# A fused recurrence and highway layer on one core: PSUM banks of the last unit, output products split in two, and a new hand-written order

## The chip, the cores and the metric

The kernel runs on one core of one Trainium2 chip. The metric is the device time of one execution in microseconds. The core has five engines that matter here: TensorE (PE; its weight loads are listed apart as PEld), VectorE (DVE), ScalarE (ACT), GpSimd (POOL) and SyncE (SP), which here only issues DMA transfers. Each engine takes its instructions strictly in the order in which they are written and waits on semaphores for what it needs.

## What is computed

The reference, cut to what matters, has two stages. The first is a gated recurrence along the sequence, for 4 sequences of 6336 steps and 256 channels:

```python
sig = 1 / (1 + exp(-f_logit))
f = lower_bound + (1 - lower_bound) * sig
h = f[:, t] * h + (1 - f[:, t]) * x[:, t]      # for each t; y[:, t] = h
```

The second is a highway layer on the 25344 x 256 result y:

```python
H = maximum(y @ w_h, 0)
T = sigmoid(y @ w_t + b_t)
out = T * H + (1 - T) * y
```

Inputs and outputs are float32. The kernel computes out as y + T * (max(y, y @ w_h ...) - y) in a rearranged form with scaled weights, in 16-bit types on the engines.

## The kernel before

The 25344 tokens are cut into 28 units: units 0 and 1 have 2 blocks of 128 tokens, unit 2 has 4, units 3 to 25 have 8, unit 26 has 4 and unit 27 has 2. The 256 channels are two halves of 128.

Nothing in the code loops over units. A long string, `order` (L48), lists tokens such as `s3.1:0`; the loop at the end (L385 to L394) takes them one by one and calls `do_` plus the letter. In `s3.1:0`, s is the step, 3 the unit, 1 the half or part, and 0 the buffer slot; `a0` and `a1` name one-bank PSUM slots, a bare 0, 1 or 2 for a product names a slot of two PSUM banks; a trailing `v` puts the step on VectorE; `*3` puts three idle matmuls ahead. All is pinned to this order on each engine, so the string fixes the order of each engine's queue and of SP's transfers. The steps of a unit are:

- l, x (L247 to L251): load logits and x, issued by SP. wt, wh: load weights. w (L380): store, issued by SP.
- u (L253, ACT): u = sigmoid(-logit) over the whole unit.
- b (L259): the product u * x in two parts; POOL, or DVE with `v`.
- i (L268, PE): transpose u to PSUM; f (L274): f = 1 - c * u from there; ACT, or DVE with `v`.
- p (L285, PE): transpose the products b to PSUM. Its one instruction set covers both parts of b.
- s (L304, DVE): the scan, y = f * y + b, each half continuing the half of the unit ahead.
- g and z (`ffn`, L312, PE): the two matmuls of the layer for one half m of the output channels; t (L331, ACT): sigmoid of z; d (L335, DVE): the maximum of g and scaled y, written as d.
- e (L340): d = d * t; POOL, or DVE with `v`. In units 7 to 21 it is one instruction, else two or three parts.
- o (L355, PE): the output product, which turns tokens back into rows: for each block and half a matmul of y with a diagonal matrix (L365) and one of d with the identity (L366), summed in PSUM. c (L369): copy to SBUF; ACT, or DVE with `v`.
- k (L224, PE): idle matmuls on zeros. cc, dg, WT, WH, cb (DVE): preparation of constants and weights. pc, pb (PE): their transposes.

The helper `shared` (L178) keeps the last product b or e (or weight preparation) of VectorE in mind, and makes the next b or e of GpSimd in the list wait for it; it makes VectorE wait for nothing.

Output products of units 24 to 26 are cut into parts of two blocks and those of unit 27 into parts of one block (`part`, L351); others have four blocks.

Of the kernel before, what the change touches and what calls it, by code (L numbers as in the profile page):

```python
# [48 lines left out]
l1:0 l0:1 x0:0 x1:1 k*3:a0 l2:2 wt wh x2:2 l3:3 x3:3 l4:4 pc:0 x4:4 u0:0 l27:1 l5:5 b0.0v:0 x27:0 x5:5 u1:1 cc l6:0
k*3:1 i0.1:0 f0.1:0 dg i1.0:1 b1.0v:1 f1.0:1 k*3:1 k*3:a0 p0.1:1 s0.1:0 i0.0:0 u2:0 f0.0v:0 p0.0:1 s0.0 x6:1 l7:2  # L50
k*3:a0 WT pb:0 k*3:a1 i2.0:0 p1.0:1 f2.0:0 WH k*3:1 s1.0:1 i2.1:0 b2.1v:0 g0.0:1 b2.0 i1.1:1 z0.1:2 f2.1:1 cb f1.1v:2
z0.0:0 g0.1:a0 p1.1:1 t0.0:0 d0.0:0 k*3:1 d0.1 p2.0:0 s1.1 k*3:0 e0.0v z1.1:1 p2.1:1 t0.1 u3:0 l8:3 g1.1:0 x7:2 s2.0:2
e0.1 d1.1:1 b3.0:0 z1.0:2 t1.0:0 i3.1:0 f3.1:0 o0.0:0 g1.0:2 c0.0:0 s2.1 d1.0 b3.1v g2.1:2 i3.0:0 d2.1:0 p3.1*3:1 t1.1
e1.1 e1.0 k*2:0 w0.0 u4:1 z2.0:1 f3.0:1 z2.1:0 b4.0:1 s3.1:0 p3.0:0 o1.0:2 t2.1:0 u27:0 b4.1 c1.0:1 s3.0 w1.0 x8:3
i4.0:1 g2.0:0 f4.0:0 d2.0 i4.1:1 p4.0:0 l9:1 x9:4 l11:4 t2.0 u5:2 e2.1v e2.0v z3.0:0 g3.1:1 b27.0:0 z3.1:2 s4.0:1
p4.1:0 f4.1:1 i5.0:1 t3.0:0 t3.1 d3.1:1 b5.0:2 g3.0:0 f5.0:0 s4.1 o2.0:1 u6:1 b5.1 c2.0:2 d3.0 w2.0 i5.1:1 x11:0 e3.2
g4.1:2 p5.0:0 d4.1:0 b6.0:1 f5.1:1 s5.0:2 z4.1:0 t4.1:1 p5.1:1 b6.1 u7:2 e3.1 s5.1 l10:0 z4.0:1 t4.0 g4.0:0 i6.0:0
e3.0v p6.0:1 d4.0 o3.0:1 e4.2 b7.0:2 f6.0:0 s6.0:3 e4.0v i6.1:0 b7.1 u8:3 f6.1:1 o3.1:0 c3.0:0 c3.1:1 w3.1 w3.0 g5.0:2
p6.1:0 i8.1:1 z5.0:1 f8.1:0 x10:1 e4.1 t5.0:0 g5.1:0 i7.1:1 b8.0:1 s6.1 i7.0:0 d5.0:1 z5.1:1 l12:2 f7.1:1 p7.1:1 d5.1
f7.0:2 t5.1 b8.1 g6.0:2 p7.0:0 e5.1 k*3:0 o4.1:1 s7.1:0 z6.0:0 d6.0:2 s7.0 u9:1 b9.0:2 g6.1:2 c4.1:3 d6.1 i9.0:1  # L60
t6.0:1 b9.1 o4.0:1 u11:2 i9.1:0 f9.0v:1 c4.0:2 w4.0 e6.0v f9.1:2 g7.1:0 z6.1:2 k*3:1 e5.2v i8.0:1 z7.0:1 e5.0v t6.1
w4.1 f8.0:3 p8.1:0 d7.1:0 t7.0:0 g7.0:2 e6.1 p8.0:1 b11.0:3 o5.0:0 u10:1 c5.0:0 w5.0 x12:2 o5.1:1 c5.1:1 w5.1 s8.1:1
i11.1:0 z7.1:0 f11.1:0 s8.0 b11.1 l13:0 d7.0 p9.0:1 i10.1:0 z8.0:1 e6.2 b10.1:1 g8.1:2 t7.1 f10.1:3 p9.1:0 s9.0:2
o6.1:0 x13:0 i10.0:1 d8.1:1 s9.1 g8.0:2 t8.0:1 u12:3 o6.0:1 f10.0:1 c6.1:0 c6.0:2 b10.0 e7.0 i11.0:1 w6.0 p10.0:0 w6.1
f11.0:2 z8.1:0 t8.1 z9.0:1 t9.0:0 d8.0 g9.0:2 s10.0:3 i12.0:1 p10.1:0 l14:1 f12.0:1 d9.0:2 o7.0:0 g9.1:1 c7.0:1 x14:1
w7.0 s10.1 u13:1 o7.1:2 c7.1:3 w7.1 b12.0:2 l17:0 p11.0:1 d9.1 s11.0:0 z9.1:0 t9.1 i12.1:0 b12.1 l15:2 z10.1:1 g10.1:2
e8.0 t10.1:2 e9.0v b13.0:1 z10.0:0 f12.1:2 p11.1:1 b13.1 t10.0 o8.1:1 d10.1:0 p12.1:0 c8.1:0 o8.0:2 s11.1 u14:2
g10.0:0 d10.0 c8.0:2 b14.1:3 i13.1:1 e10.0 f13.1:0 g11.1:1 b14.0 z11.1:0 s12.1:1 d11.1:1 w8.0 t11.1:0 x15:0 w8.1
z11.0:2 i13.0:1 p12.0:0 s12.0 o9.0:0 t11.0 f13.0:2 g11.0:1 d11.0 o9.1:2 e11.0 p13.0:1 c9.0:1 u17:1 i14.0:0 f14.0v:1
c9.1:3 g12.0:0 u15:3 d12.0:2 b15.1:2 w9.0 z12.1:1 i17.0:0 f17.0:3 t12.1:1 o10.0:2 s13.0:2 o10.1:0 p13.1:0 c10.0:0  # L70
s13.1 b15.0 c10.1:1 i14.1:1 g12.1:1 z12.0:2 g13.0:0 i15.0:0 l16:1 f14.1:2 d12.1 p14.0:1 x16:2 d13.0:0 t12.0 o11.0:1
w9.1 g13.1:2 s14.0:3 f15.0:0 p14.1:0 o11.1:0 e12.0 w10.0 w10.1 i15.1:1 c11.0:2 u16:2 x17:1 b16.1:1 b16.0 z13.0:1 d13.1
f15.1:1 c11.1:0 z13.1:2 s14.1 t13.1:0 l18:0 t13.0 w11.0 p15.0:1 o12.1:0 i16.0:0 g14.1:2 s15.0:0 d14.1:1 e13.0 o12.0:1
p15.1:1 s15.1 c12.1:1 b17.1:2 f16.0:2 z14.1:0 z14.0:2 p16.0:0 s16.0:1 c12.0:3 t14.1:1 t14.0 g14.0:1 d14.0 i16.1:1
w11.1 l19:1 u18:3 x18:0 b17.0 e14.0 g15.1:0 d15.1:2 z15.0:2 i17.1:0 x19:3 f16.1:0 b18.0:3 p16.1:1 f17.1:1 b18.1 l20:2
s16.1 o13.1:1 t15.0:0 p17.0:0 g15.0:0 w12.1 d15.0 c13.1:0 u19:1 b19.1:1 o13.0:2 p17.1:1 z15.1:1 c13.0:2 z16.0:0
s17.1:2 t15.1 t16.0:1 z16.1:2 s17.0 g16.0:1 w13.1 t16.1 i18.0:1 d16.0:0 g16.1:0 o14.0:2 i18.1:0 f18.0:0 d16.1 e15.0v
o14.1:1 p18.0:1 s18.0:3 u20:2 w12.0 z17.0:0 c14.0:0 c14.1:1 f18.1:1 g17.0:2 d17.0:1 z17.1:1 b19.0 t17.0:0 i19.1:0
f19.1:0 p18.1:1 o15.1:0 w13.0 s18.1 t17.1 x20:1 i19.0:0 l21:0 g17.1:2 e16.0 d17.1 o15.0:1 f19.0:2 b20.0:2 b20.1
p19.1:0 x21:2 w14.0 i20.1:1 c15.1:2 g18.1:0 w14.1 s19.1:0 c15.0:3 z18.0:1 f20.1:1 l22:1 o16.0:2 d18.1:2 w15.1 u21:1  # L80
t18.0:1 p19.0:0 c16.0:0 i20.0:1 g18.0:0 s19.0 f20.0:0 o16.1:1 c16.1:1 z18.1:2 i21.1:0 b21.1:1 p20.0:1 t18.1 e17.0v
d18.0 o17.0:1 w15.0 z19.1:0 b21.0 f21.1:2 g19.0:2 s20.0:1 x22:0 d19.0:0 p20.1:0 s20.1 c17.0:2 t19.1:0 o17.1:1 u22:2
e18.0 z19.0:0 g19.1:2 b22.1:2 c17.1:3 t19.0 i21.0:1 d19.1 e19.0 i22.0:0 b22.0 f21.0:0 g20.1:1 z20.1:0 l23:2 w16.0
f22.0v:1 d20.1:1 w16.1 w17.0 x23:1 p21.1:1 w17.1 l24:0 u23:1 b23.0:3 t20.1:1 o18.0:2 o18.1:1 c18.0:0 s21.1:2 c18.1:1
p21.0:0 z20.0:0 b23.1 g20.0:2 i22.1:1 x24:2 t20.0 s21.0 f22.1:2 o19.1:1 p22.1:0 d20.0 c19.1:2 e20.0 i23.1:1 z21.0:0
g21.1:1 f23.1:0 t21.0:0 u24:2 p22.0:1 g21.0:2 b24.0:1 s22.1:3 i23.0:0 d21.1:2 f23.0:2 o19.0:0 z21.1:1 b24.1 s22.0
p23.1:0 d21.0 c19.0:3 t21.1 i24.0:1 w18.1 z22.0:0 z22.1:2 g22.1:1 s23.1:0 e21.0 w18.0 f24.0:1 w19.1 d22.1:0 l25:1
i24.1:1 x25:0 t22.0:1 t22.1 f24.1:0 e22.1 p23.0:0 o20.0:0 c20.0:0 w19.0 g22.0:1 p24.1:1 o20.1:2 u25:1 b25.0:2 s23.0
b25.1 p24.0:0 c20.1:1 d22.0 z23.0:0 s24.0:1 g23.0:1 t23.0:2 e22.0 l26:0 o21.0:2 c21.0:2 o21.1:0 s24.1 i25.1:0 g23.1:2
c21.1:3 x26:1 e22.2 g24.1:0 d23.0:1 f25.1:1 u26:2 b26.0:1 i27.1:1 i25.0:0 f27.1:0 d23.1 w20.0 z23.1:1 p25.0:1 f25.0:2  # L90
d24.1:2 s25.0:2 z24.0:2 p25.1:0 b26.1 t23.1 o22.0:0 e23.1 o22.1:1 t24.0:0 e23.2 z24.1:2 c22.0:0 s25.1 w20.1 g24.0:0
d24.0 e23.0v w21.0 c22.1:1 t24.1 w21.1 e24.0 w22.0 i26.0:1 e24.1 z25.0:1 i27.0:0 f26.0:2 g25.0:2 e24.2 i26.1:1 d25.0:0
f27.0:1 t25.0:1 p26.0:0 f26.1:3 o23.0:0 g25.1:1 z25.1:2 p26.1:1 s26.0:3 d25.1 c23.0:0 s26.1 w22.1 o23.1:0 p27.0:0
t25.1 w23.0 c23.1:1 o24.0:1 e25.0v o24.3:2 s27.0:0 g26.0:a1 o24.2:0 c24.0:2 o24.1:1 d26.0:1 c24.3:0 c24.2 c24.1
p27.1:0 e25.1 e25.2v z26.0:2 o25.0:0 o25.1:1 z26.1:a1 s27.1 g26.1:a0 t26.0:0 z27.0:2 c25.0:3 t26.1 c25.1v o25.2:0
t27.0:1 o25.3:1 d26.1 g27.0:a0 w23.1 z27.1:a1 w24.1 w24.0 e26.0 c25.2:0 e26.1v o26.0:2 o26.1:0 d27.0:0 g27.1:a0 d27.1
w25.0 c25.3 t27.1 e27.0 e27.1v o27.0:1 c27.0v:1 c26.0:2 o27.1:a0 c26.1 w25.1 w26.0 w27.0 c27.1:3 w27.1
"""

    NU = len(units)  # L100
# [210 lines left out]

    def ffn(n, m, name, k, slot):  # L312
        N = tokens(n)
        p = two_banks(slot, name)
        for ki in range(NH):
            w = w_sb[:, k, ki, m * P:(m + 1) * P]
            for a in range(0, N, 512):
                e = min(a + 512, N)
                if a == 0:
                    pin(nc.tensor.matmul(p[:, a:e], w, half(n, "y", ki)[:, a:e], start=ki == 0, stop=ki == NH - 1))  # L320
# [31 lines left out]
        w = min(2 if n in (24, 25, 26,) else 4, store(n))  # L352
        return k * w, min(k * w + w, units[n][0])

    def do_o(n, k, eng, slot):  # L355
# [4 lines left out]
        for j in range(a, c):  # L360
            lo = j0 * P + j - j0
            cols = slice(lo, lo + g * (P - 1) + 1, g)
            for h in range(NH):
# [2 lines left out]
                pin(nc.tensor.matmul(o, half(n, "d", h)[:, cols], ident_b, start=False, stop=True))  # L366
# [56 lines left out]
```

## Time and profile before

| | |
|---|---|
| three runs | 207.75, 207.75 and 211.6 us, median 207.75 |
| profiled execution | 207.88 us |
| its span | 206.1 us |
| granted TensorE clock | 0.995 |

The page of a profile gives the busy time of each engine with its share of the span; a busy time is the time in which at least one instruction of the engine was running. A timeline row gives the start in us, the length in us, engine, line, operation, output and inputs with their shapes, the number of instructions merged into the row, and in brackets the idle time ahead of it with the instruction that ended it. A row of the chain that ended last starts with the start and the length. SPq is the issuing queue of SP; a row of issues gives the count, the KB of each, and the median us from issue to landing.

### The profile page before, as it was taken

How to read it: one execution, taken by the hardware profiler on the slowest of the kernel's cores; microseconds unless marked ns; L12 is line 12 of the kernel's file. 1: busy time of each engine (PE TensorE's matmuls, PEld its weight loads, DVE VectorE, ACT ScalarE, POOL GpSimd, SP SyncE). 2: the span in 40 equal slices, each digit the busy share in tenths (PEclk: the TensorE clock that was granted, in tenths of full speed). 3: DMA queues.
4: the chain of work that ended last, by engine and by line, in shares of the span. 5: the costliest groups of instructions: out<-in, count | busy, mean ns of one | idle time of the engine just before them, and what ended most of it. 6: DMA issues, size and time to landing. Idle time of an engine off the chain costs nothing.

```text
span 206.1 us, 4635 instructions
## 1 busy us (share of the span) xinstructions
PE 192.6 (93%) x1837; PEld 133.8 (65%) x1837; DVE 194.5 (94%) x159; ACT 191.9 (93%) x192; POOL 173.8 (84%) x93
## 2 busy tenths in 40 slices
...
GB/s 196 370 424 422 411 418 423 409 423 417 414 423 408 429 417 426 423 420 413 425 424 416 433 411 417 429 415 418 407 422 422 414 392 378 286 104 204 138 382 248
DMA packets 16125, 78.68 MB, mean 382 GB/s; under 512 B 1764, under 2 KB 2536, under 8 KB 10216
## 3 DMA queue, kind: packets, MB, share of 16 engines
...
q8 instruction: 14, 0.23, 0.4%
...
HBM read 52.43 MB, written 25.95 MB: 380 GB/s over the span
## 4 chain that ended last, share of the span: by engine, by line
PE 53%; ACT 14%; DMA 13%; DVE 10%; issue 6%; POOL 2%; SPq 1%; ACTq 0%; DVEq 0%; POOLq 0%
DMA x<-in_x_dram 9%; DVE y L308 8%; PE op L366 7%; PE bT L291 7%; PE op L365 7%; PE g L320 7%; PE z L320 6%; PE uT L271 6%; PE g L114 6%; PE z L114 6%; ACT o L378 4%; ACT f L282 4%; DMA out_dram<-o 4%; ACT t L333 3%; POOL bv L264 2%
## 5 line engine op out<-in xcount | busy, mean ns | idle before, releaser
L264 POOL TENSOR_TENSOR bv<-u,x 128x1024 bf16<-128x1024 f16 (+1 forms) x49 | 100.9, 2085 | 16.9 <-DVE bt L207 10.7
L308 DVE TENSOR_TENSOR_SCAN y<-f,y,bT 128x1024 bf16<-128x1024 f16 (+5 forms) x54 | 106.8, 1989 | 0.2 <-PE bT L291 0.2
L343 POOL TENSOR_TENSOR d<-d,t 128x512 bf16<-128x512 bf16 (+3 forms) x33 | 73.3, 2234 | 9.6 <-DVE d L343 4.2
L337 DVE SCALAR_TENSOR_TENSOR d<-y,ncc,g 128x1024 bf16<-128x1024 bf16 (+2 forms) x56 | 63.1, 1137 | 1.5 <-PE g L320 1.0
L333 ACT ACTIVATE t<-z,bt 128x1024 bf16<-128x1024 f32 (+2 forms) x56 | 58.9, 1088 | 1.3 <-PE z L114 0.7
L282 ACT ACTIVATE f<-uT,ncc 128x1024 f16<-128x1024 f16 (+2 forms) x51 | 55.4, 1098 | 3.4 <-PE uT L271 2.2
L378 ACT COPY o<-op 128x1024 f32<-128x1024 f32 (+2 forms) x55 | 52.1, 984 | 2.4 <-PE op L366 1.6
L256 ACT ACTIVATE u<-l 128x2048 f16<-128x2048 f32 (+2 forms) x28 | 49.8, 1781 | 2.8 <-DMA l<-in_f_logit_dram 2.7
L366 PE MATMUL op<-ident_b,d 128*128 128x128 bf16 x396 | 49.5, 219 | 0.6 <-DVE d L343 0.6
L365 PE MATMUL op<-diag,y 128*128 128x128 f16 x396 | 49.7, 219 | 0.1
L366 PEld LDWEIGHTS <-d 128*128 128x128 bf16 x396 | 44.0, 113 | 3.2 <-DVE d L343 0.7
L365 PEld LDWEIGHTS <-y 128*128 128x128 bf16 x396 | 44.2, 113 | 1.7
L320 PE MATMUL g<-y,w_sb 128*128 128x512 bf16 (+1 forms) x112 | 39.5, 367 | 0.9 <-DVE d L337 0.7
L320 PE MATMUL z<-y,w_sb 128*128 128x512 bf16 (+1 forms) x112 | 39.3, 367 | 0.4 <-ACT o L378 0.4
L291 PE MATMUL bT<-ident_f,bv 128*128 128x128 f32 x198 | 31.8, 277 | 4.3 <-DVE y L308 2.6
L114 PE MATMUL z<-y,w_sb 128*128 128x512 bf16 x92 | 34.9, 379 | 0.0
L114 PE MATMUL g<-y,w_sb 128*128 128x512 bf16 x92 | 34.9, 379 | 0.0
L320 PEld LDWEIGHTS <-w_sb 128*128 128x128 f16 x224 | 21.6, 98 | 17.5 <-issue 0.9
L271 PEld LDWEIGHTS <-u 128*128 128x128 f16 x396 | 26.3, 98 | 10.2 <-issue 2.6
L271 PE MATMUL uT<-ident_h,u 128*128 128x128 f16 x396 | 31.2, 220 | 1.6 <-DVE y L308 0.8
L291 PEld LDWEIGHTS bT<-ident_f,bv 128*128 128x128 f32 x198 | 22.4, 141 | 12.3 <-ACT f L282 3.0
L114 PEld LDWEIGHTS <-w_sb 128*128 128x128 f16 x184 | 18.0, 98 | 16.7 <-issue 1.8
...
## 6 DMA issues: line engine op xcount, KB each, us to landing
...
l<-in_f_logit_dram SPq DMA_DIRECT2D x23, 1024.0 KB, 12.0
x<-in_x_dram SPq DMA_DIRECT2D x23, 1024.0 KB, 13.4
...
```

Source lines behind the costliest of these rows:

```text
L114: return pe.add_instruction(mybir.InstMatmult(name=nc.get_next_instruction_name(), start_tensor_calc=start, stop_tensor_calc=stop, tile_si ...
L264: shared(pin(e.tensor_mul(st[n]["bv"][:, a:c].rearrange("p k d j -> p k j d"), st[n]["u"][:, 2 * a:2 * c].rearrange("p (k j) d -> p k j d" ...
L271: pin(nc.tensor.transpose(uT[:, j * P:(j + 1) * P], st[n]["u"][:, j, h * P:(h + 1) * P], ident_h))
L282: pin(nc.scalar.activation(to, of, AF.Identity, scale=ncc[:, h:h + 1], bias=1.0))
L291: pin(nc.tensor.transpose(words[:, k:k + g * (P - 1) + 1:g], pair, ident_f))
L308: pin(nc.vector.tensor_tensor_scan(y[:, c:e], st[n]["f", h][:, c:e], st[n]["bT", h][:, c:e], 0.0 if fresh else carry[h], op0=ALU.mult, op1 ...
L320: pin(nc.tensor.matmul(p[:, a:e], w, half(n, "y", ki)[:, a:e], start=ki == 0, stop=ki == NH - 1))
L333: pin(nc.scalar.activation(half(n, "t", m), st[n]["z", m][:, :tokens(n)], AF.Sigmoid, bias=bt[:, m:m + 1]))
L337: pin(nc.vector.scalar_tensor_tensor(half(n, "d", m), half(n, "y", m), ncc[:, m:m + 1], st[n]["g", m][:, :tokens(n)], op0=ALU.mult, op1=AL ...
L343: shared(pin(e.tensor_mul(st[n]["d"][:, a:c], st[n]["d"][:, a:c], st[n]["t"][:, a:c])), not eng)
L365: pin(nc.tensor.matmul(o, half(n, "y", h)[:, cols], diag[:, h], start=True, stop=False))
L366: pin(nc.tensor.matmul(o, half(n, "d", h)[:, cols], ident_b, start=False, stop=True))
```

## The change

Three things in the code:

- `ffn`: in unit 27 both halves m of a gate product (g or z) share one PSUM tile; half m takes its columns m * 256 to m * 256 + 256, so both lie in one bank. Before, each half had a tile of its own.
- A new step q holds the y matmuls of an output product in units 25, 26 and 27, and o then holds only the d matmuls; in the other units o holds both as before. The first matmul into a bank alone has the start flag in q. The loop over halves is now outside the loop over blocks, in all units.
- The string `order` is replaced by a new one. It has 829 tokens where the old has 821; the eight more are the q tokens. Engines change for some tokens: b1.0 and b2.1 go from VectorE to GpSimd, b3.0 and b4.1 from GpSimd to VectorE; e0.0, e2.0, e2.1, e4.0, e25.2 and e27.1 from VectorE to GpSimd, e1.1, e3.1, e4.1, e4.2 and e27.0 from GpSimd to VectorE; f0.1, c25.0, c25.3, c26.0 and c27.1 from ScalarE to VectorE, c25.1 from VectorE to ScalarE. All other tokens keep their engine.

The diff, with the middle of the new string left out:

```diff
+l0:0 x0:0 l1:1 x1:1 k*3:a0 wh pc:0 pb:1 l2:2 u0:0 x2:2 b0.0v:0 wt cc k*3:2 l3:3 dg x3:3 l4:0 i0.1:0 x4:0 l5:4 i0.0:1
+f0.0v:0 k*3:0 p0.0:1 u1:1 x5:4 l27:1 f0.1v:1 b1.0:1 cb k*3:a0 p0.1:0 s0.0:0 k*3:0 s0.1 i1.1:1 f1.1v:0 p1.1:0 u2:0 WH
+b2.0:0 b2.1 k*2:0 l6:5 i1.0:1 k*3:1 f1.0:1 g0.1:0 g0.0:1 p1.0:1 s1.1:1 d0.1:0 i2.0:0 s1.0 d0.0 WT f2.0:0 g1.1*2:0
+i2.1:1 d1.1:1 f2.1:1 g1.0:1 p2.0:0 z0.1:2 p2.1:1 t0.1:0 u3:0 s2.0:2 z1.0:0 z1.1:2 e0.1 d1.0 s2.1 z0.0:1 k*3:a0 i3.1:0
+b3.1v:0 b3.0v t1.0:1 i3.0:1 t1.1 e1.1v g2.1:0 t0.0 f3.1:0 p3.1*1:0 f3.0:1 d2.1:2 s3.1:3 e0.0 z2.0:1 u4:0 o0.0:0 t2.0:0
+e1.0 c0.0:0 w0.0 z2.1:2 i4.0*1:1 x6:1 p3.0:0 g2.0:0 f4.0:2 l7:0 o1.0:1 t2.1 i4.1:1 k*3:2 c1.0:1 b4.1v:1 b4.0 s3.0 x7:2
+f4.1:0 u5:1 w1.0 l8:2 k*3:1 d2.0 p4.0:1 e2.1 z3.1:1 t3.1:1 g3.1:0 s4.0:0 z3.0:2 d3.1:0 e2.0 p4.1:0 i5.0:1 s4.1 u27:0
+b5.1:0 g3.0:1 x8:3 l9:3 d3.0 o2.0:0 b5.0 e3.2 e3.1v t3.0 e3.0v f5.0:1 u6:2 i5.1:1 p5.0:0 g4.1:2 c2.0:0 w2.0 f5.1:0
+x9:0 b6.0:1 s5.0:1 z4.1:1 t4.1:0 d4.1:1 o3.0:0 c3.0:2 u7:1 i6.0:1 g4.0:1 f6.0:1 p5.1:0 w3.0 o3.1:0 z4.0:2 s5.1 b6.1
+i6.1:1 c3.1:1 d4.0 w3.1 p6.0:0 f6.1:0 g5.0:0 t4.0 l11:0 p6.1:1 s6.0:2 k*3:1 s6.1 b7.1:0 z5.0:2 u8:2 b7.0 x11:1 i7.0:0
+t5.0:1 z5.1:1 e4.0 g5.1:2 d5.0:0 l10:1 b8.1:1 t5.1 b8.0 d5.1 g6.0:1 d6.0:2 e5.2v e4.1v e5.0v x27:4 p7.0:1 e4.2v f7.0:0
+u9:3 s7.0:3 i8.1:0 z6.1:0 g6.1:2 f8.1:1 x10:5 i7.1:0 z6.0:1 t6.1:2 f7.1:2 o4.1:0 l12:4 t6.0 i8.0:0 d6.1 c4.1:0 b9.1:2
+f8.0:0 p7.1:1 s7.1 o5.1:1 o4.0:0 c5.1:1 i9.0:0 f9.0v:2 c4.0:2 b9.0 w4.0 e6.1 w4.1 e6.2 e6.0v e5.1 k*3:2 z7.1:1 p8.0:1
+w5.1 s8.0:0 u11:1 i9.1:0 g7.1:0 d7.1:1 z7.0:2 b11.0:0 b11.1 f9.1:3 b27.0:3 p8.1:0 t7.1:0 t7.0 s8.1 x12:0 g7.0:1 d7.0
+u10:2 o5.0:2 i11.1:1 o6.1:0 p9.0:0 f11.1:0 s9.0:1 c5.0:3 i10.1:1 f10.1:1 z8.0:1 g8.1:2 w5.0 t8.0:1 l13:0 i10.0:1
...
+c22.1:1 b26.1 t24.1 z25.0:1 e23.1 p26.0:0 g25.0:2 e23.2 f27.0:0 i26.0:1 z25.1:0 e23.0v d25.0:0 t25.0:1 g25.1:1 f26.0:1
+s26.0:2 i26.1:1 o23.0:2 w21.0 e24.0 w21.1 p26.1:0 t25.1 o23.1:0 d25.1 f26.1:3 p27.0:1 e24.1 w22.0 c23.0:0 s26.1
+o24.0:1 e24.2 c23.1:2 s27.0:3 o24.1:2 w22.1 g26.0:a0 c24.0:1 e25.0v o24.2:0 p27.1:1 o24.3:1 c24.1 c24.2:3 g26.1:2
+d26.0:1 z26.0:a0 s27.1 d26.1 c24.3 q25.1:0 w23.0 t26.0:0 q25.0:a1 e25.1 o25.1 o25.0 e25.2 q25.3:1 z26.1:a0 w23.1
+c25.0v:0 o25.3 c25.1 w24.0 q25.2:0 e26.0 c25.3v:2 t26.1 g27.1:2 o25.2 w24.1 z27.1:a1 c25.2 e26.1v z27.0 d27.1:0
+q26.0:a0 w25.0 q26.1:1 t27.1:0 o26.0 w25.1 t27.0 c26.0v:1 o26.1 g27.0 e27.1 d27.0 q27.1:0 e27.0v c26.1 q27.0:a1 o27.1
+c27.1v:0 w26.0 o27.0 w27.1 c27.0v:3 w27.0
...
     def ffn(n, m, name, k, slot):
         N = tokens(n)
-        p = two_banks(slot, name)
+        if n in (27,):
+            if name not in st[n]:
+                st[n][name] = two_banks(slot, name)
+            p = st[n][name][:, m * N:(m + 1) * N]
+        else:
+            p = two_banks(slot, name)
...
-    def do_o(n, k, eng, slot):
-        op = two_banks(slot, "op").rearrange("p (j d) -> p j d", d=D)
+    def outputs(n, k, op):
         a, c = part(n, k)
         j0, j1 = blocks(n, a // store(n))
         g = j1 - j0
-        for j in range(a, c):
-            lo = j0 * P + j - j0
-            cols = slice(lo, lo + g * (P - 1) + 1, g)
-            for h in range(NH):
-                o = op[:, j - a, h * P:(h + 1) * P]
-                pin(nc.tensor.matmul(o, half(n, "y", h)[:, cols], diag[:, h], start=True, stop=False))
-                pin(nc.tensor.matmul(o, half(n, "d", h)[:, cols], ident_b, start=False, stop=True))
+        for h in range(NH):
+            for j in range(a, c):
+                lo = j0 * P + j - j0
+                yield (h, j) == (0, a), (h, j) == (NH - 1, c - 1), op[:, j - a, h * P:(h + 1) * P], h, slice(lo, lo + g * (P - 1) + 1, g)
+
+    def do_q(n, k, eng, slot):
+        op = two_banks(slot, "op").rearrange("p (j d) -> p j d", d=D)
+        for first, _, o, h, cols in outputs(n, k, op):
+            pin(nc.tensor.matmul(o, half(n, "y", h)[:, cols], diag[:, h], start=first, stop=False))
+        st[n]["op", k] = op
+
+    def do_o(n, k, eng, slot):
+        if n in (25, 26, 27,):
+            for _, last, o, h, cols in outputs(n, k, st[n]["op", k]):
+                pin(nc.tensor.matmul(o, half(n, "d", h)[:, cols], ident_b, start=False, stop=last))
+            return
+        op = two_banks(slot, "op").rearrange("p (j d) -> p j d", d=D)
+        for _, _, o, h, cols in outputs(n, k, op):
+            pin(nc.tensor.matmul(o, half(n, "y", h)[:, cols], diag[:, h], start=True, stop=False))
+            pin(nc.tensor.matmul(o, half(n, "d", h)[:, cols], ident_b, start=False, stop=True))
         st[n]["op", k] = op
```

77 lines of the change are left out of this document (28 added, 49 removed).

## The prediction

> **What bounds the kernel now.** I read the page first (engine totals), then busy time by stage, then VectorE's timeline, because the totals point at it, and last the issues and the queue of SP. Columns of the stage row: PE, PEld, DVE, ACT, POOL busy, granted clock, DMA share, GB/s.
>
> ```profile
> PE 192.6 (93%) x1837; PEld 133.8 (65%) x1837; DVE 194.5 (94%) x159; ACT 191.9 (93%) x192; POOL 173.8 (84%) x93
> 30.00:170.00 140.00, 135.19 (x1324) 95.58 (x1323) 139.43 (x92) 139.58 (x128) 132.87 (x57) 1.00 1.02 418
> ```
>
> The second line is the argument: from 30 to 170 us DVE stands still for only 140.00 - 139.43 = 0.57 us and ACT for 0.42 us, while DMA is full too. DVE's queue never runs dry, so what is added to DVE before the tail is added to the end, and what is taken from it is taken from the end, unless a gap appears or closes. ACT loses work by the change, so I sum on DVE: time to its first work, its instructions, its waits, and what follows the last. The profiled execution took 207.88 us for a span of 206.1, so 1.8 us lie around the span; the median of the runs shown is 207.75, 0.13 less. The matmul count and the warming matmuls of the k tokens (35 in each list) stay, apart from one more on another token, so PE's total stays.
>
> Here are the rows of DVE from which prices come. A step is the start of the next row less the start of this one, since neighbours overlap by some 0.1 us.
>
> ```profile
> 5.52 0.73 DVE L264 TENSOR_TENSOR bv<-u,x 128x512 bf16<-128x512 f16 x1 [4.39 <-DMA x<-in_x_dram]
> ...
> 12.06 0.71 DVE L264 TENSOR_TENSOR bv<-u,x 128x512 bf16<-128x512 f16 x1
> 12.67 0.14 DVE L207 COPY bt<-tbT 128x2 f32<-128x2 f32 x1
> 12.73 0.47 DVE L280 TENSOR_SCALAR f<-uT,ncc 128x256 f16<-128x256 f16 x1
> 13.12 0.89 DVE L337 SCALAR_TENSOR_TENSOR d<-y,ncc,g 128x256 bf16<-128x256 bf16 x2
> ...
> 14.59 0.27 DVE L343 TENSOR_TENSOR d<-d,t 128x256 bf16<-128x256 bf16 x1
> 14.78 1.27 DVE L308 TENSOR_TENSOR_SCAN y<-f,y,bT 128x512 bf16<-128x512 f16 x1
> ...
> 17.96 1.75 DVE L264 TENSOR_TENSOR bv<-u,x 128x1024 bf16<-128x1024 f16 x1
> 19.61 0.73 DVE L337 SCALAR_TENSOR_TENSOR d<-y,ncc,g 128x512 bf16<-128x512 bf16 x1
> 20.33 4.58 DVE L308 TENSOR_TENSOR_SCAN y<-f,y,bT 128x1024 bf16<-128x1024 f16 x2
> 24.83 0.72 DVE L337 SCALAR_TENSOR_TENSOR d<-y,ncc,g 128x512 bf16<-128x512 bf16 x1
> 25.47 0.78 DVE L343 TENSOR_TENSOR d<-d,t 128x512 bf16<-128x512 bf16 x2
> 26.17 2.34 DVE L308 TENSOR_TENSOR_SCAN y<-f,y,bT 128x1024 bf16<-128x1024 f16 x1
> ...
> 42.76 0.67 DVE L343 TENSOR_TENSOR d<-d,t 128x1024 bf16<-128x1024 bf16 x1
> 43.34 2.34 DVE L308 TENSOR_TENSOR_SCAN y<-f,y,bT 128x1024 bf16<-128x1024 f16 x1
> ```
>
> Steps: b of 512 elements 0.61; f of 256 0.39; e of 256 0.19, of 512 0.35 (0.70 for two), of 1024 0.58; d of 512 0.72 and 0.64; two scans 4.50, so 2.25 each; b of 1024 1.65. That last price is doubtful, as two more products of this form come to DVE:
>
> ```profile
> 12.91 1.17 POOL L264 TENSOR_TENSOR bv<-u,x 128x512 bf16<-128x512 f16 x1 [10.67 <-DVE bt L207]
> 15.00 0.68 POOL L343 TENSOR_TENSOR d<-d,t 128x256 bf16<-128x256 bf16 x1 [0.92 <-DVE d L343]
> 16.40 2.14 POOL L264 TENSOR_TENSOR bv<-u,x 128x1024 bf16<-128x1024 f16 x1 [0.72 <-DMA x<-in_x_dram]
> ...
> 21.39 4.25 POOL L264 TENSOR_TENSOR bv<-u,x 128x1024 bf16<-128x1024 f16 x2 [0.23 <-DMA x<-in_x_dram]
> ```
>
> POOL's own product of the same unit ran until 16.40 + 2.14 = 18.54, across the first 0.58 us of DVE's 1.75. Twice the 512 step is 1.22; 1.22 + 0.58 would be 1.80, near the 1.75. So I price a 1024 product at 1.2 where POOL is quiet, with 1.65 as its other end.
>
> The Trainium skill, "SBUF — State Buffer", section "Who interferes with whom", says that a VectorE instruction with two SBUF inputs and a GpSimd instruction that reads SBUF exclude each other for the whole instruction. By that rule DVE begins at 18.54 and the sum takes 1.2, which the 0.58 us above agrees with; if the rule did not act here the sum would take 1.65.
>
> **Start, up to the scans of unit 3.** The new list issues l0, x0 ahead of l1, x1. So x0 is SP's second issue and not its third:
>
> ```profile
> 1.16 0.42 SPq L244
> ...
> 1.63 3.79 DMA x<-in_x_dram
> ```
>
> Issued at 1.16 with the same 3.79 us, x0 lands at 4.95, and DVE begins 0.5 us earlier than 5.52. From its start to b3.1v DVE spent 17.96 - 5.52 = 12.44. On this stretch the new list takes b1.0, b2.1 and e0.0 off DVE (0.61 + 0.61 + 0.19 = 1.41) and puts f0.1 on it (0.39): 11.42, so b3.1v would come at 16.4 (4.95 + 11.42). The other end: the first f and p steps pass PE behind more k groups, and the loads land as before; 0.6 us more gives 17.0. Earlier than 16.40 is excluded: x3, still the tenth load, is what POOL's row at 16.40 waited for. I take 16.4. b1.0, b2.0 and b2.1 now run on POOL, which stood idle until 12.91; b1.0 waits there for the dg instructions and b2.0 for those of WH, since the new list puts those just ahead, and p2.0 follows. That is the work most likely to add the 0.6.
>
> Then b3.1v and b3.0v, both on DVE. POOL is quiet: the next product there, e0.0, stands behind e1.1v, for which the helper makes it wait. 16.4 + 1.2 + 1.2 + 0.19 (e1.1v) + 0.72 (d2.1) = 19.7 for s3.1, against 20.33 before: -0.6. With 1.65 twice it is 20.6, +0.3.
>
> **Units 3 to 6.** DVE gains b4.1v (1.2) and e3.1v, e4.1v, e4.2v (3 x 0.35 = 1.05), and loses e2.1, e2.0 (0.70) and e4.0 (0.58): +0.97, or +1.42 at the dear price. What is queued behind b4.1v: x4 landed by 21.39, b4.1v comes at 19.7 + 2.25 = 21.95, so no load holds it. b4.0 on POOL now waits for b4.1v: 21.95 + 1.2 = 23.15, plus half of POOL's 4.25 for two, gives 25.3, and p4.0 follows. DVE covers this with s3.0 (2.25) and d2.0 (0.64), until 26.04; 0.7 us of cover for the transposes, half of it needed. If u4 is late, each us of it goes through to s4.0. Sum to unit 7: -0.6 + 0.97 = +0.35 (ends +0.3 and +2.3: 17.0 for 16.4, 1.65 three times).
>
> **Middle.** Units 7 to 24 have the same DVE instructions in another order. The gaps can shrink by 0.57 at most. To the other side the nearest rows are DVE's waits in the tail below, of which the longest is 0.78; two such are 1.6. I take 0, since every token here keeps its engine. The order of output products is now half by half in all units; the same matmuls in another order, and each is covered by the DVE row beside it; without cover it would show as one such wait.
>
> **Tail.** Rows of DVE from s26.1, and the last copy on ACT:
>
> ```profile
> 192.98 1.27 DVE L308 TENSOR_TENSOR_SCAN y<-f,y,bT 128x512 bf16<-128x512 f16 x1
> 194.17 0.66 DVE L343 TENSOR_TENSOR d<-d,t 128x1024 bf16<-128x1024 bf16 x1
> 194.75 0.73 DVE L308 TENSOR_TENSOR_SCAN y<-f,y,bT 128x256 bf16<-128x256 f16 x1
> 195.41 0.72 DVE L337 SCALAR_TENSOR_TENSOR d<-y,ncc,g 128x512 bf16<-128x512 bf16 x1
> ...
> 197.35 0.69 DVE L376 COPY o<-op 128x512 f32<-128x512 f32 x1 [0.23 <-PE op L366]
> ...
> 199.06 0.42 DVE L343 TENSOR_TENSOR d<-d,t 128x512 bf16<-128x512 bf16 x1
> 199.61 0.48 DVE L337 SCALAR_TENSOR_TENSOR d<-y,ncc,g 128x256 bf16<-128x256 bf16 x1
> 200.87 0.48 DVE L337 SCALAR_TENSOR_TENSOR d<-y,ncc,g 128x256 bf16<-128x256 bf16 x1 [0.78 <-PE g L320]
> 201.46 0.29 DVE L343 TENSOR_TENSOR d<-d,t 128x256 bf16<-128x256 bf16 x1
> 202.07 0.43 DVE L376 COPY o<-op 128x256 f32<-128x256 f32 x1 [0.32 <-PE op L366]
> ```
>
> ```profile
> 202.63 0.37 ACT L378 COPY o<-op 128x256 f32<-128x256 f32 x1 [1.30 <-PE op L366]
> ```
>
> From s26.1 to the end of the last copy: 203.00 - 192.98 = 10.02. Removed: the 0.78, in which g27.1 waited for the bank that d27.0 was reading (both had slot a0). In the new list both gate products share slot 2, and g27.0 stands behind o26.1. Added to DVE: three copies net (c25.0, c25.3, c26.0 and c27.1 for c25.1); e25.2 leaves for POOL. New DVE sequence: s26.1 1.19, e25.0 0.58, s27.0 0.66, s27.1 0.66, d26.0 and d26.1 0.67 each, c25.0, c25.3 and c26.0 0.69 each, e26.1 0.42, d27.1 and d27.0 0.48 each, e27.0 0.29, c27.1 and c27.0 0.43 each: 9.03. Waits that stay: 0.32 for the last output product and one like the 0.23 where c25.3 follows e25.2 on POOL. Sum 9.6: -0.4. The y products issued ahead leave only the d products after the last e; but that 0.32 is mostly the first product's way, so I cut nothing for them. Ends: -0.9 with no waits (9.03), and +0.4 if the 0.78 comes back elsewhere.
>
> The Trainium skill, "PSUM — Partial Sum Buffer", section "PSUM bank collisions raise a hardware error", has accesses of two engines kept apart by bank, not by address. That speaks against one bank for both halves: g27.0 must then follow d27.1's read, and t27.1 must follow z27.0. No row here shows a bank shared in this way.
>
> By rows: d27.1 follows e26.1 on DVE and takes 0.48, about as long as o26.0 and o26.1 need on PE after the same e26.1, so g27.0 loses at most some tenths; the +0.4 end holds it.
>
> **Sum.** 207.88 + 0.35 + 0 - 0.4 = 207.83, taken as 207.8, which is 0.05 above the median of the runs.
>
> **The rivals.** (1) Slower, by the price of DVE's products and by the start: a 1024 product costs 1.65 whether or not POOL reads, and PE's early groups cost 0.6. For it: 1.65 is the only measured step. Against it: the 512 steps. 207.88 + 2.3 - 0.4 = 209.8; it decides against the forecast from a product of some 1.5 us on. (2) Slower by more: SP, in order, now has store w0.0 ahead of load x6, where ten further loads stood ahead of it.
>
> ```profile
> 13.82 0.33 SPq L244 DMA_DIRECT2D l<-in_f_logit_dram  x1
> ...
> l<-in_f_logit_dram SPq DMA_DIRECT2D x23, 1024.0 KB, 12.0
> x<-in_x_dram SPq DMA_DIRECT2D x23, 1024.0 KB, 13.4
> ```
>
> The issue at 13.82 is l6; what is in flight then lands 12.0 to 13.4 us later, at about 26. SP stands until c0.0 on ACT is done, which needs e0.0 on POOL (after e1.1v, so 19.0 + 0.68) and stands behind u4 and t2.0.
>
> ```profile
> 18.77 1.91 ACT L256 ACTIVATE u<-l 128x2048 f16<-128x2048 f32 x1
> 20.59 1.10 ACT L282 ACTIVATE f<-uT,ncc 128x1024 f16<-128x1024 f16 x1
> ```
>
> u4 was at 18.77; the new list puts f3.0 (1.10) ahead of it, so it ends near 21.7 (18.77 + 1.10 + a step of 1.82), and t2.0 and c0.0, each half as wide as that f, bring c0.0 to 23 or 24. Below 26 the queue keeps DMA full; beyond it each us is a us without loads, felt by DVE once b6 is late. The same pattern returns with w3.1 and w5.0 ahead of loads. With c0.0 at 31, or two holes of half that, 207.8 + 5 = 212.8. (3) Faster: the new order closes the 0.57 and the tail's waits: 207.88 + 0.3 - 0.57 - 0.9 = 206.7. (4) The shared bank and the early y products do nothing, as the last e still ends the chain: tail 0, 208.2.
>
> **How the numbers follow.** Forecast 0.45 (own range 207.2 to 208.6, holding rival 4 too, 0.08), rival 1 0.18, rival 2 0.13, rival 3 0.16. The range 206.4 to 210.8 takes in all but rival 2 and the tips of 1 and 3. Two per cent, about what a measurement of this kernel can tell from no change, is 4.2 us: 203.6 and 211.9. Faster than 203.6 would need more than all the gaps here: 0.03. Slower than 211.9 is rival 2 and a part of rival 1: 0.14. Within: 0.83.
>
> **What would show it.** In the new profile: DVE's first product near 5.0; b3.1v at 16.4 to 17.0, the two products there at 1.25 us each and s3.1 near 19.7; DVE idle from 30 to 170 us below 1.2; SP's issue of x6 before 26 and DMA share 1.0 to 170; some 9.6 us from s26.1 to the last copy, with no wait of 0.78 before a d of 256. Wrong if DVE shows a gap in the middle, above all one ended by a load or by POOL's b; then the queue's order decided and not DVE's sum.

## The result, and the profile after

The changed kernel takes 210.25 us (median of 4 runs, 209.97 to 210.44) against 207.99 for the kernel before, taken beside it: ratio 1.0108, 95% interval 1.0093 to 1.0123. It is slower by 1.1%: inside the range and inside two per cent, but 2.45 us above the 207.8 forecast. With an interval 0.3% wide, far less than the two per cent that the prediction allowed can be told from no change here. The profiled execution took 209.97 us with a span of 208.0, 1.9 more than the 206.1 of before.

The engine totals and the stage from 30 to 170 us, columns as before:

```profile
PE 192.8 (93%) x1811; PEld 134.0 (64%) x1838; DVE 197.1 (95%) x162; ACT 191.0 (92%) x188; POOL 173.9 (84%) x94
```
```profile
30.00:170.00 140.00, 134.28 (x1298) 95.19 (x1317) 139.89 (x94) 139.81 (x128) 132.20 (x55) 1.00 1.02 418
```

DVE's gaps in the middle shrank from 0.57 to 0.11 us, and nothing new opened there. A gap doesn't show a row that has grown, so the place of the loss is read from the starts of rows. DVE's start:

```profile
4.16 0.73 DVE L265 TENSOR_TENSOR bv<-u,x 128x512 bf16<-128x512 f16 x1 [3.03 <-DMA x<-in_x_dram]
...
16.40 2.47 DVE L265 TENSOR_TENSOR bv<-u,x 128x1024 bf16<-128x1024 f16 x2
18.75 0.29 DVE L349 TENSOR_TENSOR d<-d,t 128x256 bf16<-128x256 bf16 x1
...
19.68 2.35 DVE L309 TENSOR_TENSOR_SCAN y<-f,y,bT 128x1024 bf16<-128x1024 f16 x1
21.95 1.30 DVE L265 TENSOR_TENSOR bv<-u,x 128x1024 bf16<-128x1024 f16 x1
23.16 2.32 DVE L309 TENSOR_TENSOR_SCAN y<-f,y,bT 128x1024 bf16<-128x1024 f16 x1
25.41 0.71 DVE L343 SCALAR_TENSOR_TENSOR d<-y,ncc,g 128x512 bf16<-128x512 bf16 x1
26.44 2.35 DVE L309 TENSOR_TENSOR_SCAN y<-f,y,bT 128x1024 bf16<-128x1024 f16 x1 [0.32 <-PE bT L292]
```

b3.1v at 16.40, the two products in 2.35 (1.18 each), s3.1 at 19.68 and b4.1v at 21.95 are where the forecast had them. The miss begins in the last row, at s4.0, which waits for p4.0. The tail:

```profile
193.68 1.91 DVE L309 TENSOR_TENSOR_SCAN y<-f,y,bT 128x512 bf16<-128x512 f16 x2
...
199.21 0.69 DVE L394 COPY o<-op 128x512 f32<-128x512 f32 x1 [1.09 <-DMA out_dram<-o]
200.54 0.69 DVE L394 COPY o<-op 128x512 f32<-128x512 f32 x1 [0.63 <-ACT t L339]
...
204.09 0.76 DVE L394 COPY o<-op 128x256 f32<-128x256 f32 x2 [0.66 <-DMA out_dram<-o]
```
```profile
199.19 0.59 ACT L396 COPY o<-op 128x512 f32<-128x512 f32 x1 [0.92 <-DMA out_dram<-o]
```
```profile
198.86 0.39 PE L379 MATMUL op<-ident_b,d 128*128 128x128 bf16 x4
```

Three copies, c25.0v, c25.1 on ACT and c27.1v, wait by these rows for a store, not for a product. The 0.63 ahead of c25.3v is probably a fourth wait of this kind, though its row names a sigmoid: its product o25.3 (the PE row) was done at 199.25, and its buffer, slot 2, waits for the store w23.1, issued at 195.1. s26.1 starts 0.70 us later than before (193.68 against 192.98); from there to the last copy it takes 204.85 - 193.68 = 11.17 us against 10.02 (+1.15); from the last copy to the end of the span 3.15 against 3.1. That is the whole 1.9. The chain of work that ended last runs through two of these waits, both for one buffer:

```profile
192.97 1.03 ACT o L396
...
194.02 5.08 DMA out_dram<-o
...
199.21 0.70 DVE o L394
...
199.97 4.03 DMA out_dram<-o
...
204.09 0.09 DVE o L394
```

The third part of a token c is the slot of the output buffer in SBUF, 0 to 3. c23.0 fills slot 0 and its store w23.0 takes 5.08 us; c25.0v has slot 0 too; its store w25.0 takes 4.03; c27.1v has slot 0 again. In the old list the buffers went round in another order (c24.3 had slot 0, c25.0 slot 3, c27.0 slot 1).

My theory after this: (a) the tail is late by these buffers, (b) the start by the 0.39 us at s4.0 and the products added to DVE, which nothing behind it gives back. Rivals: the waits for stores stand only ahead of other waits; the store w0.0 ahead of x6 starves the loads; ACT or the loads, as full as DVE, set the pace.

### The profile page after: what moved, and what is told of

Same layout as the page of the kernel before. It is cut to its first block, busy times and chain, and to the rows that moved or that the text cites. A ratio compares the mean times of both kernels' runs of the same rounds, so it can differ in the third digit from the quotient of the medians.

```text
span 208.0 us, 4611 instructions
## 1 busy us (share of the span) xinstructions
PE 192.8 (93%) x1811; PEld 134.0 (64%) x1838; DVE 197.1 (95%) x162; ACT 191.0 (92%) x188; POOL 173.9 (84%) x94
## 4 chain that ended last, share of the span: by engine, by line
PE 40%; DVE 24%; ACT 17%; issue 11%; DMA 4%; POOL 1%; DVEq 0%; ACTq 0%; POOLq 0%; SPq 0%
DVE y L309 15%; PE bT L292 6%; ACT u L257 5%; PE z L326 5%; PE g L326 5%; PE uT L272 5%; PE op L383 4%; DMA out_dram<-o 4%; PE op L384 4%; PE z L115 4%; ACT f L283 4%; DVE d L343 4%; ACT o L396 4%; PE g L115 3%; ACT t L339 3%
## 5 line engine op out<-in xcount | busy, mean ns | idle before, releaser
L265 POOL TENSOR_TENSOR bv<-u,x 128x1024 bf16<-128x1024 f16 (+1 forms) x49 | 98.8, 2049 | 16.9 <-DVE d L349 5.4
L349 POOL TENSOR_TENSOR d<-d,t 128x512 bf16<-128x512 bf16 (+3 forms) x34 | 75.3, 2229 | 11.5 <-ACT f L283 4.3
L339 ACT ACTIVATE t<-z,bt 128x1024 bf16<-128x1024 f32 (+2 forms) x56 | 56.6, 1050 | 2.0 <-PE z L115 1.0
L396 ACT COPY o<-op 128x1024 f32<-128x1024 f32 (+1 forms) x52 | 49.5, 970 | 2.0 <-DMA out_dram<-o 0.9
L383 PE MATMUL op<-diag,y 128*128 128x128 f16 x368 | 45.9, 219 | 0.2
L384 PE MATMUL op<-ident_b,d 128*128 128x128 bf16 x368 | 45.8, 219 | 0.0
L384 PEld LDWEIGHTS <-d 128*128 128x128 bf16 x368 | 41.0, 114 | 2.5 <-issue 0.6
L383 PEld LDWEIGHTS <-y 128*128 128x128 bf16 x368 | 41.1, 113 | 2.1
L115 PE MATMUL z<-y,w_sb 128*128 128x512 bf16 x83 | 31.4, 379 | 0.0
L115 PE MATMUL g<-y,w_sb 128*128 128x512 bf16 x78 | 29.6, 379 | 0.0
```

The source lines that it names most:

```text
L115: return pe.add_instruction(mybir.InstMatmult(name=nc.get_next_instruction_name(), start_tensor_calc=start, stop_tensor_calc=stop, tile_si ...
L265: shared(pin(e.tensor_mul(st[n]["bv"][:, a:c].rearrange("p k d j -> p k j d"), st[n]["u"][:, 2 * a:2 * c].rearrange("p (k j) d -> p k j d" ...
L339: pin(nc.scalar.activation(half(n, "t", m), st[n]["z", m][:, :tokens(n)], AF.Sigmoid, bias=bt[:, m:m + 1]))
L349: shared(pin(e.tensor_mul(st[n]["d"][:, a:c], st[n]["d"][:, a:c], st[n]["t"][:, a:c])), not eng)
```

## The experiments

Kernels that build on another differ from it by the lines shown. The runs stand on several chips, each with the kernel before beside it, so times are compared by their ratio to it. "Own buffers" is this edit of the changed kernel, with copies of units 25 to 27 in load buffers that are free by then:

```diff
-c25.0v:0 ... c25.3v:2 ... c26.0v:1 ... c27.1v:0 ... c27.0v:3
+c25.0v:4 ... c25.3v:5 ... c26.0v:6 ... c27.1v:7 ... c27.0v:8
...
+            spare = {"4": "x3", "5": "x4", "6": "x5", "7": "l3", "8": "l4"}
+            if slot in spare:
+                st[n]["o", j0] = pool.tile([P, NB, D], FP32, tag=spare[slot], name="o")
+            else:
+                st[n]["o", j0] = sb([P, 4, D], FP32, "o", slot)
```

**Own buffers.**

> The changed kernel, but the copies of units 25 to 27 write into five output buffers of their own (load buffers that are free by then) and not into the four that all units share. Theory: the tail is late because c25.0, c25.1 and c27.1 wait until an earlier store has emptied their buffer (1.09 and 0.66 us of DVE, 0.92 of ACT in the changed profile). Without these waits, from s26.1 to the last copy takes about 9.6 us and not 11.17, and the time is near 208.7 us, ratio to before 1.002 to 1.005. Rival: the waits for stores only stand in front of others (the d products of unit 25 on GpSimd, the sigmoids of unit 26), and the stretch stays at 10.7 or more: 209.8 us, ratio above 1.008.

Measured 209.45 us, ratio 1.0060 (1.0038 to 1.0081): its interval lies below that of the change. DVE in its tail:

```profile
193.53 1.90 DVE L310 TENSOR_TENSOR_SCAN y<-f,y,bT 128x512 bf16<-128x512 f16 x2
...
198.26 0.69 DVE L399 COPY o<-op 128x512 f32<-128x512 f32 x1 [0.28 <-PE op L380]
199.13 0.69 DVE L399 COPY o<-op 128x512 f32<-128x512 f32 x1 [0.19 <-PE op L380]
...
200.91 0.69 DVE L399 COPY o<-op 128x512 f32<-128x512 f32 x1 [0.36 <-PE op L380]
...
202.76 0.76 DVE L399 COPY o<-op 128x256 f32<-128x256 f32 x2 [0.38 <-PE op L380]
```

No row shows a wait for a store any more, the wait ahead of c25.3v fell from 0.63 to 0.19, and s26.1 to the last copy takes 203.52 - 193.53 = 9.99, 1.18 less. But the span fell by only 0.7, to 207.3: the gap from the last copy to the end grew from 3.15 to 3.8. The theory has the waits right and the time too low; where the rest stays is in the stores:

```profile
190.00:194.00 4.00, 4.00 (x51) 3.17 (x50) 4.00 (x5) 3.52 (x5) 3.80 (x3) 1.00 0.00 0
194.00:198.00 4.00, 3.95 (x54) 3.21 (x52) 3.97 (x6) 3.60 (x6) 2.39 (x3) 1.00 0.74 287
198.00:204.00 6.00, 3.93 (x54) 3.30 (x51) 4.23 (x9) 3.22 (x7) 2.26 (x3) 1.00 1.02 406
```

DMA (share and GB/s in the last two columns) stands idle for 4 us, is busy for 0.74 of the next 4 and full from 198 to 204. In the kernel before its share from 190 to 194 was not 0 but 0.33:

```profile
190.00:194.00 4.00, 4.00 (x49) 3.09 (x46) 4.00 (x4) 3.09 (x4) 4.00 (x3) 1.00 0.33 131
```

**Own buffers, without the two stores of unit 24** (`-w24.0`, `-w24.1`; 1 MB of output is not written).

> The kernel with own output buffers (e1_more_out) without the two stores of unit 24: 1 MB of the output is not written. Theory: with own buffers the end is set by the stores, which keep DMA full from 198 us on: the last copy ends 3.8 us ahead of the span's end where it was 3.1 in both kernels. Without this 1 MB the gap goes back to 3.1 or less: span 206.6 or below and 208.5 us. Rival: the gap is fixed by the last store's own way, and the span stays at 207.2 to 207.4.

Measured 208.73 us, ratio 1.0012 (0.9983 to 1.0040). In the profiled execution s26.1 stood at 194.21, and the last copy ends at 204.20:

```profile
203.44 0.76 DVE L399 COPY o<-op 128x256 f32<-128x256 f32 x2 [0.38 <-PE op L380]
```

The span is 207.1, so the gap is 2.9: back to 3.1 or less, as the theory wants, though the span itself isn't 206.6 since this execution was late from the start. So the stores' backlog is part of the end; the next run, just as late, gives its size.

**Own buffers, y products no longer ahead** (each q right ahead of its o).

> The kernel with own output buffers (e1_more_out), but in units 25 to 27 each group of y matmuls stands right ahead of its d matmuls again, so nothing is issued ahead. Theory: the early y products are worth one or two tenths, since after the last product on VectorE only two y matmuls more stand in the way; from s26.1 to the last copy 10.0 to 10.3 us against 9.99. Rival, they matter: each of the waits of VectorE for an output product (0.28, 0.19, 0.36, 0.38 us) grows, 10.6 us or more.

```profile
194.20 1.90 DVE L310 TENSOR_TENSOR_SCAN y<-f,y,bT 128x512 bf16<-128x512 f16 x2
...
203.40 0.76 DVE L399 COPY o<-op 128x256 f32<-128x256 f32 x2 [0.38 <-PE op L380]
```

204.16 - 194.20 = 9.96 against 9.99, 209.51 us, ratio 1.0031 (0.9998 to 1.0064). Issuing y products ahead is worth nothing that can be seen here: 0.38 us ahead of the last copies in both.

This execution also fits the one without the stores of unit 24: s26.1 at 194.20 against 194.21, the last copy until 204.16 against 204.20. Its span is 208.1 against 207.1, and the medians, taken side by side, are 209.51 and 208.73. So with DVE's work at the same times, 1 MB of stores is worth 1.0 us of the end.

**Own buffers, unit 27 with a PSUM tile for each half** (`z27.0:0`, `g27.0:a0`, and `ffn` as before).

> The kernel with own output buffers (e1_more_out), but each half of the gate products of unit 27 in a PSUM tile of its own, as before (z27.0 in slot 0, g27.0 in slot a0). Theory: g27.0 waits until c26.0 has emptied a0, so d27.0 comes later by 0.3 to 0.5 us, and z27.0 waits for c25.2 with o26.0 behind it: from s26.1 to the last copy 10.4 to 10.9 us against 9.99. Rival, sharing a bank is worth nothing: 10.0 to 10.1 us.

```profile
193.58 1.90 DVE L310 TENSOR_TENSOR_SCAN y<-f,y,bT 128x512 bf16<-128x512 f16 x2
...
201.57 0.69 DVE L394 COPY o<-op 128x512 f32<-128x512 f32 x1 [0.97 <-PE op L375]
202.73 0.48 DVE L339 SCALAR_TENSOR_TENSOR d<-y,ncc,g 128x256 bf16<-128x256 bf16 x1 [0.47 <-PE g L322]
...
203.99 0.75 DVE L394 COPY o<-op 128x256 f32<-128x256 f32 x2 [0.38 <-PE op L375]
```

204.74 - 193.58 = 11.16, more than the 10.4 to 10.9 expected: both waits appear, and the one ahead of c26.0 is the larger. So the shared bank is worth 1.2 us on this stretch, in this order and against these slots. Of that, 0.4 reach the span (207.7 against 207.3), and the time shows nothing: 209.64, ratio 1.0058 (1.0026 to 1.0089) against 1.0060. The gap to the end is 2.96 here and 3.8 with the shared bank; the stores take back what DVE gains.

**The kernel before, with one bank for g of unit 27 alone.**

```diff
-g27.0:a0 w23.1 ... d27.0:0 g27.1:a0 d27.1
+g27.0:a0 g27.1 w23.1 ... d27.0:0 d27.1
...
+        if n == 27 and name == "g":
+            if name not in st[n]:
+                st[n][name] = two_banks(slot, name)
+            p = st[n][name][:, m * N:(m + 1) * N]
```

> The kernel before with one edit: both halves of the g product of unit 27 lie in one PSUM bank, and g27.1 stands right behind g27.0, ahead of d27.0 (the old list and code otherwise). Theory: the wait of 0.78 us ahead of the last d goes, so from s26.1 to the last copy it takes 9.2 to 9.4 us and not 10.02; the stores keep DMA full to about 204 us in the profile of before, so not all of it reaches the end: 207.5 to 207.9 us against 208.2, ratio 0.997 to 0.999. Rival: the stores alone set the end, ratio 1.000 or above, with a longer gap from the last copy to the end of the span than 3.1 us.

208.39 us, ratio 1.0004 (0.9988 to 1.0020).

```profile
193.27 1.27 DVE L310 TENSOR_TENSOR_SCAN y<-f,y,bT 128x512 bf16<-128x512 f16 x1
...
200.12 0.87 DVE L344 SCALAR_TENSOR_TENSOR d<-y,ncc,g 128x256 bf16<-128x256 bf16 x2 [0.34 <-PE g L327]
```
```profile
202.44 0.37 ACT L385 COPY o<-op 128x256 f32<-128x256 f32 x1 [0.60 <-PE op L373]
```

The 0.78 is gone, the stretch is 202.81 - 193.27 = 9.54 instead of 10.02, and the span's end comes 3.9 us after the last copy instead of 3.1. (In this execution s26.1 stood 0.29 later than before.) The rival was right: the old tail too ends by its stores, so nothing is won. The -0.4 of my tail, had it come true, would hardly have reached the time either.

**b4.0 ahead of b4.1v in the list of the changed kernel.**

```diff
-b4.1v:1 b4.0
+b4.0:1 b4.1v
```

> The changed kernel with b4.0 (GpSimd) ahead of b4.1v (VectorE) in the list, so that b4.0 doesn't wait for b4.1v. Theory, two products with both inputs in SBUF exclude each other: b4.0 starts near 21.4 us, b4.1v is issued at 21.95 and ends only some 1.2 us after b4.0 has ended (near 24.8; it shows 2.8 us and not 1.3), s3.0 and s4.0 come some 1.1 us later: 211.3 us, ratio about 1.016. Rival, they run side by side: b4.1v takes 1.3 to 1.7 us, p4.0 is ready earlier and the wait of 0.32 us ahead of s4.0 goes: 209.9 us, ratio 1.009 or less.

```profile
22.05 2.47 DVE L266 TENSOR_TENSOR bv<-u,x 128x1024 bf16<-128x1024 f16 x1
24.42 2.33 DVE L310 TENSOR_TENSOR_SCAN y<-f,y,bT 128x1024 bf16<-128x1024 f16 x1
```
```profile
21.21 2.15 POOL L266 TENSOR_TENSOR bv<-u,x 128x1024 bf16<-128x1024 f16 x1 [0.62 <-ACT u L258]
```

b4.1v takes 2.47 us where it took 1.30. POOL's product ends at 23.36; 23.36 - 22.05 = 1.31 of standing still and 1.2 of work are 2.5. So the two exclude each other, and DVE's row shows the wait as length, not as idle time. s4.0 came 0.87 later (27.31). Yet the time was 209.98, ratio 1.0072 (1.0046 to 1.0097), not 1.016: the theory had the mechanism and missed the time. s26.1 was 0.74 late, but from there to the last copy it took 10.58 and not 11.17, as the wait of c25.0v for its buffer shrank from 1.09 to 0.49. That part of the tail was waiting anyway.

**Own buffers, with e3.1, e4.1, e4.2 on GpSimd as before** (the `v` taken off three tokens).

> The kernel with own output buffers (e1_more_out) with e3.1, e4.1 and e4.2 on GpSimd as before and not on VectorE. Theory: VectorE, never idle from 30 to 170 us, has 3 x 0.35 = 1.05 us less to do, so s26.1 starts 1.0 us earlier (192.5 against 193.5) and the time is 0.6 to 1.0 us lower: 208.5 to 208.9 us, ratio 1.001 to 1.004. Rival: GpSimd, which gets 3 x 1.17 = 3.5 us more, makes VectorE wait for the products b of the next units, or ACT, as full as VectorE, holds the pace: s26.1 at 193.2 or later and no gain.

211.12 us, ratio 1.0110 (1.0050 to 1.0170): no gain, the rival's side, but by another way than it said. Whether it is slower than own buffers alone (1.0060) the overlapping intervals don't settle. DVE lost 1.05 us of work, and s26.1 came 1.5 us later (195.03), of which 0.23 stood there ahead of the edit (b4.1v at 22.20 against 21.97). The largest single step, 0.95 us, is at e9.0v, first in this kernel with the POOL row beside it, then with own buffers alone:

```profile
82.03 2.20 DVE L350 TENSOR_TENSOR d<-d,t 128x2048 bf16<-128x2048 bf16 x1
```
```profile
80.95 2.20 POOL L266 TENSOR_TENSOR bv<-u,x 128x1024 bf16<-128x1024 f16 x1
```
```profile
81.55 1.25 DVE L350 TENSOR_TENSOR d<-d,t 128x2048 bf16<-128x2048 bf16 x1
```

With more work ahead, POOL's b comes 1.4 us later and lies across the first 1.12 us of e9.0v, until 83.15; to the next row of DVE it is 2.12 us. With own buffers alone POOL's b was nearly done when e9.0v began (at 81.72), and to the next row it is 1.17.

**Own buffers, with b4.1 on GpSimd as before** (`b4.1:1`).

> The kernel with own output buffers (e1_more_out) with b4.1 on GpSimd as before, and so both products of unit 4 there one behind the other. My prediction's reading, VectorE's sum sets the time: VectorE has 1.2 us less to do, s26.1 starts at 192.3 to 192.6 and not 193.5, the time falls to 208.5. Rival, the product was free on VectorE: GpSimd ends b4.0 at about 25.5, p4.0 follows by 26.2, so s4.0 starts at 26.3 as before with a wait of 1.4 us ahead of it; GpSimd is 2.1 us later for the products of unit 5, so s5.0 comes later than 34.3 and s26.1 at 193.5 to 194.5: no gain, 209.4 us or above.

209.33 us, ratio 1.0056 (1.0032 to 1.0079): no gain, the rival. Its profiled execution was the slowest of its eight (210.58) and had a late load:

```profile
22.92 4.24 POOL L266 TENSOR_TENSOR bv<-u,x 128x1024 bf16<-128x1024 f16 x2 [2.07 <-DMA x<-in_x_dram]
```
```profile
23.22 2.35 DVE L310 TENSOR_TENSOR_SCAN y<-f,y,bT 128x1024 bf16<-128x1024 f16 x1 [0.82 <-PE bT L293]
...
27.97 2.35 DVE L310 TENSOR_TENSOR_SCAN y<-f,y,bT 128x1024 bf16<-128x1024 f16 x1 [1.76 <-PE bT L293]
```

What b4.1 no longer takes on DVE comes back as waits for p: s3.0 came at 23.22, against 23.14 with own buffers alone. The 1.76 ahead of s4.0 holds the late load too. With GpSimd's products 1.5 us earlier, at the 21.39 of the kernel before, s4.0 would come at about 26.4, an estimate, against 26.45 with own buffers alone. So around s4.0 the chain of x4, the products and p4.0 sets the time, not DVE's sum.

**Own buffers, with e20.0 on VectorE** (one product more in the middle).

> The kernel with own output buffers (e1_more_out) with the product e20.0 (2048 elements) on VectorE and not on GpSimd: VectorE has 1.25 us more in the middle, GpSimd 4.1 us less. Theory, VectorE without a gap passes every delay on to the end: s26.1 starts 1.2 us later than without the edit in an execution with the same start (more if the product finds GpSimd busy), 210.4 to 211 us, ratio 1.010 to 1.014. Rival, the loads or ACT, just as full, set the pace and VectorE has hidden room: 209.3 to 209.7 us, ratio 1.006.

210.19 us, ratio 1.0088 (1.0055 to 1.0122), a little below the expected 1.010 to 1.014. Its interval overlaps that of own buffers alone (1.0060), so the rows have to tell.

```profile
164.87 2.34 DVE L310 TENSOR_TENSOR_SCAN y<-f,y,bT 128x1024 bf16<-128x1024 f16 x1
167.13 1.20 DVE L350 TENSOR_TENSOR d<-d,t 128x2048 bf16<-128x2048 bf16 x1
...
176.29 4.59 DVE L310 TENSOR_TENSOR_SCAN y<-f,y,bT 128x1024 bf16<-128x1024 f16 x2
```

Ahead of the product this execution ran 0.11 us earlier than own buffers alone (its scan there stands at 164.98), and the scan at 176.29 came 1.02 later than there (175.27): 1.13 us passed on in full. At s26.1 the 1.02 was 0.81: e23.0 took 0.69 us here and 1.07 with own buffers alone, where a product of POOL lay across it. In the middle DVE does set the pace.

**The kernel before, with l0, x0 ahead of l1, x1.**

> The kernel before with one edit: l0, x0, l1, x1 are issued in this order, as in the new list. Theory: VectorE starts near 4.2 us and not 5.5, but at b3.1v it meets the landing of x3 and GpSimd's own product of that unit, which started when x3 landed; VectorE's product is held until GpSimd has ended (near 18.5 to 19) and shows 2 us or more, so that s3.1 starts at 20.0 to 20.5 as before: 208.0 to 208.4 us, ratio 0.999 to 1.001. Rival: the 1.3 us gained at the start are kept, s3.1 at 19.0 to 19.3, ratio 0.996 or less.

```profile
4.61 0.73 DVE L266 TENSOR_TENSOR bv<-u,x 128x512 bf16<-128x512 f16 x1 [3.48 <-ACT u L258]
...
18.03 1.86 DVE L266 TENSOR_TENSOR bv<-u,x 128x1024 bf16<-128x1024 f16 x1
...
20.49 4.59 DVE L310 TENSOR_TENSOR_SCAN y<-f,y,bT 128x1024 bf16<-128x1024 f16 x2
```

208.17 us, ratio 1.0020 (0.9988 to 1.0052): an earlier first product is worth nothing in the old list. But not as I expected: the 0.9 us were gone by b3.1v already, mostly in a wait of 0.93 us for p at the first scan.

**Two kernels of parts of both lists.** Both tell little, since the parts did not fit together.

> The new list up to the scan s4.0, then everything that is left in the order of the old list, with the old code (so the old tail). Theory: the new start gains and loses about the same; s4.0 starts 0.3 us later than before (26.44 against 26.17) and the rest is as before: 208.1 us, ratio 1.000 to 1.003. Rival: the store w0.0 ahead of the load x6 in the queue of SP, which is in this kernel, leaves a hole in the loads that the later units pay for: 0.7 us or more, ratio 1.004 or above.

229.87 us, ratio 1.1017 (1.0977 to 1.1058). The old order wants b27.0 ahead of b5.0, the new start loads x27 late: POOL stood still for 14.6 us. The price of the new start alone stays unmeasured.

> The old list up to d26.0, then the new list's tail (early y products, both halves in one bank, copies on VectorE) with the five output buffers of their own. Theory: s26.1 stands where it stood before (192.98 us), the tail takes 9.6 instead of 10.02: 207.4 to 207.6 us, ratio 0.997 to 0.999. Rival: early y products and shared banks are worth nothing without the rest, the tail takes 10.0 or more: 207.9 us or above, ratio 1.000 or above.

209.33 us, ratio 1.0052 (1.0030 to 1.0074). s26.1 stood at 192.93 as meant, but the tail took 11.67: DVE waited 0.42 us for p27.1, now behind other PE work, and 0.77 ahead of d26.1, where the row names no engine (g26.1 stands behind other work too). It does not compare the two tails.

## Why the prediction was right and where it was wrong

- **As a whole: inside a wide range, not where it was aimed.** 210.25 lies above the forecast's own range (207.2 to 208.6). It is nearest to the 209.8 of rival 1, but not by that rival's mechanism.
- **Start: right in time, in part by luck.** The forecast for b3.1v, s3.1 and b4.1v was met within 0.02 us. DVE began at 4.16 and not 4.95, and then waited for PE (0.17 at the first f, 0.56 between the first two scans); the two errors cancelled. Nor is 16.40 a floor for b3.1v: with e20.0 on VectorE it came at 16.28. The price of 1.2 for a product with POOL quiet holds (1.18); rival 1 with its 1.65 falls. The rule of the Trainium skill that the prediction cites ("SBUF — State Buffer", section "Who interferes with whom"), by which such a product of VectorE and a product of GpSimd contend, agrees with the 2.47 us and the 2.20 us above.
- **Units 3 to 6: the step that failed is "0.7 us of cover for the transposes, half of it needed".** b4.0 started when b4.1v had ended, as forecast, but at 23.48 and not 23.15, and p4.0 let s4.0 start 0.39 us later than d2.0 left DVE (26.44 against 25.41 + 0.64). The cover was 0.42, from b4.0's end at 25.63 to 26.05, and p4.0 needed 0.81. A further 0.2 us went ahead of f9.0v. At the d7.0 of both lists DVE is 0.82 us behind, and not 0.35 (64.31 against 63.49).
- **Middle: right.** From +0.82 to +0.70 at s26.1.
- **The premise, "what is taken from it is taken from the end", holds one way only.** Work added to DVE in the middle was passed on (e20.0: 1.13 us). Work taken off it was not: the time fell neither without e3.1, e4.1 and e4.2 nor without b4.1. The prediction excepted gaps that appear, and with b4.1 gone they did; a row held up by GpSimd, as e9.0v was, it did not except.
- **Tail: the step that failed is "Waits that stay: 0.32 ... and one like the 0.23".** It followed engines and PSUM and left out the output buffers in SBUF, whose slots stand in the new list. They cost 1.18 us of the stretch, as own buffers show; without them it takes 9.99 and not 9.6. There the other waits were four of 1.21 us together, where the sum had 0.55, and the instructions took about 8.8 us and not 9.03. The sum of -0.4 became +1.15. The shared bank held nothing up there: g27.0 began on PE at 200.93, after d27.1 had ended at 200.54, without a wait.
- **A thing the sum did not hold at all:** what lies behind the last copy was taken as a constant 3.1 us. It is 2.8 to 3.9 in these runs, and the stores of the last units, which fill DMA from 198 us on, are a part of it. So in the time, own buffers got back about half of the loss (1.0108 to 1.0060). Of the span's 1.2 us that are left with them, 0.55 are there at s26.1 and 0.7 lie behind the last copy.
- **Rival 2** did not happen: SP did hold x6 behind w0.0 from 11 to 22.5 us, but the loads in flight kept DMA full (a share of 1.02 from 20 to 30 us).

```profile
10.01 1.01 SPq L245 DMA_DIRECT2D l<-in_f_logit_dram  x2
22.06 0.35 SPq L400 DMA_DIRECT2D out_dram<-o  x1
22.51 0.38 SPq L245 DMA_DIRECT2D x<-in_x_dram  x1
```
```profile
20.00:30.00 10.00, 9.20 (x76) 5.79 (x77) 9.68 (x7) 9.69 (x12) 7.00 (x6) 1.00 1.02 415
```

- **Rival 4**, that the early y products and the shared bank do nothing: true of the first (9.96 against 9.99), not of the second on its stretch (11.16 against 9.99), but nearly so in the time.
- **Open:** why the stores begin later than before. In the new list o23.0 stands on PE behind z25.1 and g25.1, and c23.0 starts at 192.97 where it was 190.66, with DMA idle from 190 to 194; that this costs the 0.7 us behind the last copy is argued from the rows, and no run changes that order alone. The price of the new start alone is open too. No version here is faster than the kernel before.
